# A chunked-attention and low-rank-mixer kernel: values of one tile and scores of the next issued together in shared PSUM banks

## The chip, the cores and the metric

One Trainium2 chip, one of its cores. The metric is the device time of one execution in microseconds (us); less is better. The core has five engines that run side by side and wait for each other through semaphores: TensorE (PE: matmuls; PEld is its weight load, which overlaps them), VectorE (DVE), ScalarE (ACT), GpSimd (POOL) and SyncE (SP, which here only issues DMAs). Matmul results land in PSUM, eight banks of 128 partitions by 512 floats; everything else lies in SBUF.

## The reference

```python
# attention within chunks of 64 positions; q, k, v are (8, 8, 576, 64)
scores = (q_c @ k_c.T) / sqrt(64)
scores = scores - max(scores, axis=-1)
attn = exp(scores)
attn = attn / (sum(attn, axis=-1) + 1e-9)
x = attn @ v_c                        # as (8, 576, 512): batch, seq, heads * dim

# mixer on x
h = x.transpose @ U @ V               # over the 576 positions, rank 32
u = x + h.transpose
out = u + relu(u @ w_ch1) @ w_ch2     # 512 -> 2048 -> 512
```

U, V, w_ch1 and w_ch2 arrive as float64 and are turned into pairs of shorter numbers (a high part and the rest), so that a product is made of three or four matmuls.

## The kernel before

**Tiles.** The batch is cut into four pairs of batch entries (`pr` = 0 to 3). A pair has 1152 rows, which are nine tiles (`t` = 0 to 8) of 128 rows. There are 36 tiles; a tile has two chunks of 64 rows (`c`) and eight heads, which are four head pairs (`hp`) of two (`e`).

**Attention of a tile** (`attention_ops`, line 367). Six groups of operations: load q, k, v; `tq`, `cq`: four TensorE transposes of q into a bank (L375) and their copy to SBUF on ScalarE (L385); `tk`, `ck`: the same for k; `sc`, `m0`, `s0`, `m1`, `s1`, `ex`: the scores (L393), for each `e` maximum (L407) and subtraction (L411) on VectorE, exp on ScalarE (L415); `te`, `ce`: transposes of the exp tile and their copy; `av`, `sm`, `x0`, `x1`: the values (L424), the sums (L436, L437) and the scaled results (L442) that make the tile's `x`.

Scores and values are 32 matmuls each, one for every `(hp, e, c)` of `BLOCKS`. Each uses a quarter of the TensorE array: 64 contraction rows (chosen by `e`) by 64 output columns (chosen by `c`). All other matmuls of the kernel use the whole 128 by 128 array. Scores go to two banks, one for each `e`; values go to two other banks. v has a 65th column of ones, set by a POOL memset (L346), so that the values' 65th output column is the row sum of the exps.

**Mixer.** `project_ops` (xh, xl, y) forms x.transpose @ U for one batch entry from five tiles; `mix_ops` (u, x, ut, uth, utl) adds the low-rank part and transposes; then, for each group `g` of three tiles and each of 16 slices `f` of the 2048 hidden columns, `hidden` (L567, twelve matmuls), `relu_high` on ScalarE (L575), `relu_low` on VectorE (L580) and `project_out` (L593, nine matmuls in three flushes `j`).

**What sets the order.** Pair 0, and tiles 0 and 1 of pair 1, are placed by a planner (`order`). From there on the loop over `plan()` (line 757) writes the order: for each `(pr, g)` it runs the 16 slices and lays a list of steps (attention of later tiles, projections, mixes) evenly between the flushes. `attend` (line 718) makes the attention steps of a list of tiles. Within one list the transposes of the previous tile's exps and its values stand between the steps of the next tile; at the end of each list the last tile's `te` and `av` steps close it:

```python
steps += [ahead, step(*q)] + ([prev[0]] if prev else [])
steps += [step(*k)] + ([prev[1]] if prev else []) + [step(*sc)]
...
return steps + (list(prev) if prev else [])
```

The instructions that result need not stand in the order of these lines: the builder places an instruction on its engine when its own estimate of the run says that what it needs is there, the earlier line first. Buffers with the tag `slot` (eight) hold q, k, v, their transposes, the exps and xh, xl; `bank` has eight, of which three hold the running sums of `project_out`.

Of the kernel before, what the change touches and what calls it, by code (L numbers as in the profile page):

```python
# [10 lines left out]
F32 = mybir.dt.float32  # L11
# [4 lines left out]
AX = mybir.AxisListType  # L16
# [5 lines left out]
def kernel(  # L22
# [11 lines left out]
    nc = tc.nc  # L34
    B, H, S, D = q.shape
# [4 lines left out]
    P = 128  # L40
    C = 64
    D1 = D + 1
    HP = H // 2
    NCC = DM // P
    NF = DF // P
    NT = 2 * S // P
# [2 lines left out]
    NX = 10  # L49
    NS = 8  # L50
    XROOM = 3
    BLOCKS = [(hp, e, c) for hp in range(HP) for e in range(2) for c in range(2)]
    GN = GT * P
    NG = NT // GT
# [6 lines left out]
    work = ctx.enter_context(tc.tile_pool(name="work", bufs=1))  # L61
# [4 lines left out]
    def bank(name):  # L66
        return psum.tile([P, 512], F32, tag="bank", name=name)

    def slot(dtype, name, shape=(P, 512)):
        return work.tile(list(shape), dtype, tag="slot", name=name, bufs=NS)  # L70
# [209 lines left out]
    def w_ops(f, after=None):  # L280
# [10 lines left out]

        n = 1 if f < NF - XROOM else 2
        size = 2 * DM // n
# [33 lines left out]
    def early(pr, t):  # L327
        return pr == 0 and t < NEARLY

    loaded = {}  # L330
    begun = {}
    x_of = {}
    y_of = {}
    ut_of = {}

    def load_qk(pr, t):
        n = f"{pr}_{t}"
        if early(pr, t):
            words = wslot((4 * DM,), F32, "qkv_" + n)
            qn, kn = (words[:, z * DM : (z + 1) * DM].rearrange("p (h d) -> p h d", h=H) for z in range(2))  # L340
            vn = words[:, 2 * DM : 2 * DM + H * D1].rearrange("p (c a k) -> p c a k", c=2, k=D1)
        else:
            qn = slot(F32, "qn_" + n, (P, H, D))
            kn = slot(F32, "kn_" + n, (P, H, D))
            vn = slot(F32, "vn_" + n, (P, 2, HP, D1))
        nc.gpsimd.memset(vn[:, :, :, D:], 1.0)  # L346
        for r, m, b, s0 in segments(pr, t):
            nc.sync.dma_start(qn[r : r + m], q[b, :, s0 : s0 + m, :].rearrange("h s d -> s h d"))
            nc.sync.dma_start(kn[r : r + m], k[b, :, s0 : s0 + m, :].rearrange("h s d -> s h d"))
        loaded[pr, t] = qn, kn, vn  # L350
# [16 lines left out]
    def attention_ops(pr, t, after=None):  # L367
        n = f"{pr}_{t}"
        st = {}
# [7 lines left out]
        def evacuate(name):  # L377
            if name[0] == "e" or not mine:
                dst = slot(F32, name + n, (P, HP, P))
            elif name[0] == "q":  # L380
                st["qk"] = wslot((2, HP, P), F32, "qkT_" + n)
                dst = st["qk"][:, 0]
            else:
                dst = st["qk"][:, 1]
            nc.scalar.copy(dst.rearrange("p a b -> p (a b)"), st[name])  # L385
            st[name] = dst

        def scores():
            ps = [bank(f"sc{e}_{n}") for e in range(2)]
            for hp, e, c in BLOCKS:  # L390
                rows = slice(e * C, (e + 1) * C)
                cs = slice(c * C, (c + 1) * C)
                nc.tensor.matmul(  # L393
                    ps[e][cs, hp * C : (hp + 1) * C],
                    lhsT=st["qT_"][rows, hp, cs],
                    rhs=st["kT_"][rows, hp, cs],
                    start=True,
                    stop=True,
                )
            st["sc"] = [p[:, 0 : HP * C].rearrange("p (h k) -> p h k", k=C) for p in ps]  # L400
# [12 lines left out]
        def exp():  # L413
            exf = st["ex"].rearrange("p a b k -> p (a b k)")
            nc.scalar.activation(exf, exf, AF.Exp, scale=SCALE)  # L415

        def values():

            vn = loaded[pr, t][2]
            ps = [bank(f"av{e}_{n}") for e in range(2)]  # L420
            for hp, e, c in BLOCKS:
                rows = slice(e * C, (e + 1) * C)
                cs = slice(c * C, (c + 1) * C)
                nc.tensor.matmul(  # L424
                    ps[e][cs, hp * D1 : (hp + 1) * D1],
                    lhsT=st["eT_"][rows, hp, cs],
                    rhs=vn[rows, c, hp, :],
                    start=True,
                    stop=True,
                )  # L430
            st["av"] = [p[:, 0 : HP * D1].rearrange("p (h k) -> p h k", k=D1) for p in ps]
# [7 lines left out]
        def scaled(e):  # L439
            if e == 0:  # L440
                st["x"] = work.tile([P, HP, 2, D], F32, tag="x", name="x_" + n, bufs=NX)
            nc.vector.tensor_mul(  # L442
                st["x"][:, :, e, :],
                st["av"][e][:, :, 0:D],
                st["sm"][:, e].unsqueeze(2).broadcast_to([P, HP, D]),
            )
            if e == 1:
                x_of[pr, t] = st["x"].rearrange("p a b k -> p (a b k)")
# [3 lines left out]
        lq = Op("SP", 2.5, lambda: load_qk(pr, t), after, take="w" if mine else "slot slot slot", lat=2.2)  # L452
        lv = Op("POOL" if mine else "SP", 4.0 if mine else 2.5, lambda: load_v(pr, t), lq, lat=2.2)
        tq = Op("PE", 0.35, lambda: transpose(src(0), "qT_"), lq, begun.get((pr, t - 2)), take="bank")
        cq = Op("ACT", 0.58, lambda: evacuate("qT_"), tq, take="w" if mine else "slot", free="bank")
        tk = Op("PE", 0.35, lambda: transpose(src(1), "kT_"), lq, tq, take="bank")
        ck = Op("ACT", 0.58, lambda: evacuate("kT_"), tk, cq, take="" if mine else "slot", free="bank")
        sc = Op("PE", 0.62, scores, ck, take="bank bank", free="w" if mine else "slot slot slot slot")
        m0 = Op("DVE", 0.41, lambda: maximum(0), sc, take="slot mx")
        s0 = Op("DVE", 0.41, lambda: subtract(0), m0, free="bank")  # L460
        m1 = Op("DVE", 0.41, lambda: maximum(1), s0)
        s1 = Op("DVE", 0.41, lambda: subtract(1), m1, free="bank mx")
        ex = Op("ACT", 0.63, exp, s1)
        te = Op("PE", 0.35, lambda: transpose(flat(), "eT_"), ex, take="bank", free="slot")
        ce = Op("ACT", 0.58, lambda: evacuate("eT_"), te, take="slot", free="bank")
        av = Op("PE", 0.65, values, ce, lv, take="bank bank x", free="slot w" if mine else "slot slot")
        sm = Op("DVE", 0.5, sums, av, take="sm")
        x0 = Op("DVE", 0.415, lambda: scaled(0), sm, free="bank")
# [176 lines left out]

    LEAD = "T0 T1 U T2 T3 T4 P0 V W0 M0 T5 W1 T6 T7 W2 T8 P1 M1 W3 W4 W5 W6 W7 W8 W9 W10 W11 W12 W13 W14 W15 M2"
    STRETCHES = ((0, 0, 2), (1, 0, 4), (0, 2, 8), (1, 4, 12), (0, 8, 16), (1, 12, 16))
    GATES = (14, 29)
    BASE = 1000
    u_done = None  # L650
    v_done = []
# [25 lines left out]
    prev = None  # L677
    blocks = 0
    gates = dict(zip(GATES, range(len(GATES))))
    for g, f0, f1 in STRETCHES:  # L680
        for f in range(f0, f1):
            rank[0] = BASE
            prev = block_ops(0, g, f, f == f0, f == f1 - 1, [*w_done[f], *mixed[g]], prev)
# [31 lines left out]
    def step(*group):  # L715
        return lambda: [o.run() for o in group]

    def attend(ts):
        steps = []
        prev = None  # L720
        for key in ts:
            i = tiles.index(key)
            _, q, k, sc, et, av = attention_ops(*key)

            def ahead(i=i):
                if i + 1 < len(tiles) and tiles[i + 1] not in loaded:
                    load(*tiles[i + 1])

            steps += [ahead, step(*q)] + ([prev[0]] if prev else [])
            steps += [step(*k)] + ([prev[1]] if prev else []) + [step(*sc)]  # L730
            prev = step(*et), step(*av)
        return steps + (list(prev) if prev else [])

    def mixes(pr, ts):
        steps = []
        st = [[step(*z) for z in mix_ops(pr, t, None, [None, None])] for t in ts]
        for i in range(len(st) + 1):
            steps += ([st[i][0]] if i < len(st) else []) + ([st[i - 1][1]] if i else [])
        return steps

    def proj(pr, e):
        return [step(*z) for z in project_ops(pr, e, [None] * NT)[0]]

    def plan():
        n1 = len(GATES)
        for pr in range(NPAIR):
            nxt = [] if pr == NPAIR - 1 else [(pr + 1, t) for t in range(NT)]
            if pr > 0:
                yield pr, 0, attend([(pr, t) for t in range(7, NT)]) + proj(pr, 1) + mixes(
                    pr, range(3, 6)  # L750
                ) + attend(nxt[:1])
                yield pr, 1, mixes(pr, range(6, 9)) + attend(nxt[1:4])
            yield pr, 2, attend(nxt[n1 if pr == 0 else 4 : 5]) + ([] if not nxt else proj(pr + 1, 0)) + attend(nxt[5:7]) + (
                [] if not nxt else mixes(pr + 1, range(3))
            )

    for pr, g, steps in plan():
        done = 0
        slots = 0
        for f in range(NF):  # L760
            ps = hidden(pr, g, f)
# [43 lines left out]
```

## Time and profile before

| | before |
|---|---|
| median of 3 runs | 1030.82 us |
| range of the runs | 1030.47 to 1032.12 us |
| span of the profiled execution, first to last instruction | 1032.0 us |
| attention tiles from pair 1, tile 2 on | 25 |
| PE matmuls | 7032 |

The profiled execution's time is its span of 1032.0 us; the page gives no other for it. It lies 1.2 us above the median of the runs and within their range.

How to read it: the page gives the busy time of each engine, the span in 40 slices with the busy share in tenths, the chain of work that ended last, and groups of instructions by line. In a row of groups, `L393 PE MATMUL sc<-kT,qT 64*64 64x64 f32 x864 | busy, mean ns | idle before` means line 393, TensorE, output sc from kT and qT, 64 rows by 64 columns of the array, a 64x64 moving operand, 864 times. A row of the timeline gives start, length, engine, line, operation and how many in a row. A matmul's end is modelled, and matmuls overlap, so what matters on TensorE is the distance between starts. `[0.28 <-ACT ex L415]` behind a row says that the engine sat idle that long before it and who ended the wait.

### The profile page before, as it was taken

To read this page: it belongs to the slowest core of one execution; us is meant where nothing else is said; L and a number is where in the kernel's file an instruction comes from. 1 tells how busy PE (TensorE), PEld (TensorE's weight loads), DVE (VectorE), ACT (ScalarE), POOL (GpSimd) and SP (SyncE) were. 2 spreads that over 40 slices of the span, in tenths; PEclk is the share of its full clock that TensorE was granted. 3 is DMA by queue.
4 is the path that set the end of the run, shared out by engine and by line. 5 is a ranking of instruction groups with operands and counts; after the bars stand their busy time and mean duration, and the time that the engine had idled before them with its cause. 6 is when DMAs were issued, how large, how long until landed. Compare 5 with 4: busy or idle time off the path is not lost.

```text
span 1032.0 us, 16637 instructions
## 1 busy us (share of the span) xinstructions
PE 980.7 (95%) x7032; PEld 862.0 (84%) x7032; DVE 419.5 (41%) x834; ACT 260.8 (25%) x467; POOL 26.4 (3%) x78
## 2 busy tenths in 40 slices
PE   5486999999999999999999999999999999999998
PEld 4364888888888888988888888988888889999997
DVE  3498999973333342322423242322333332211211
ACT  3453234322322222222222222222222231111110
POOL 7100000000000000000000000000000000000000
PEclk9667899999999999999999999999999999999999
DMA  9952142305121211021021210111121000000000
GB/s 187 217 184 88 42 113 82 103 34 129 34 63 31 63 31 32 34 55 37 32 62 32 62 32 10 53 34 43 48 53 41 31 1 1 31 1 1 31 1 30
DMA packets 123157, 56.40 MB, mean 55 GB/s; under 512 B 107276, under 2 KB 115724, under 8 KB 123084
## 3 DMA queue, kind: packets, MB, share of 16 engines
q1 hardware_dynamic: 121932, 52.99, 20.1%
q0 software_dynamic: 1152, 2.36, 1.2%
q8 instruction: 55, 0.90, 0.4%
q14 instruction: 18, 0.15, 0.0%
HBM read 45.83 MB, written 9.51 MB: 54 GB/s over the span
## 4 chain that ended last, share of the span: by engine, by line
PE 69%; DVE 0%; ACT 0%; DVEq 0%; issue 0%; ACTq 0%
PE h L567 30%; PE o L593 30%; PE av L424 1%; PE sc L393 1%; PE ut L535 1%; PE ps_eT L375 1%; PE ps_kT L375 1%; PE ps_qT L375 1%; PE u L523 1%; PE y L496 1%; PE y L495 1%; DVE x L605 0%; DVE ex L411 0%; ACT ex L415 0%; DVEq L800 0%; DVE mx L407 0%
## 5 line engine op out<-in xcount | busy, mean ns | idle before, releaser
L567 PE MATMUL h<-uth,w 128*128 128x384 f32 x1536 | 427.1, 342 | 4.9 <-ACT w L308 2.1
L593 PE MATMUL o<-w,hh 128*128 128x512 f32 x1152 | 364.3, 403 | 0.6 <-ACT hh L575 0.6
L567 PEld LDWEIGHTS h<-uth,w 128*128 128x128 f32 x1536 | 282.4, 189 | 13.8 <-ACT w L308 2.6
L580 DVE SCALAR_TENSOR_TENSOR hl<-h,hh 128x384 fp32r<-128x384 f32 x192 | 106.8, 556 | 430.4 <-ACT hh L575 430.4
L567 PE MATMUL h<-utl,w 128*128 128x384 f32 x768 | 260.2, 339 | 0.4 <-DVE utl L548 0.4
L593 PEld LDWEIGHTS o<-w,hh 128*128 128x128 f32 x1152 | 207.8, 189 | 35.8 <-ACT hh L575 0.9
L593 PE MATMUL o<-w,hl 128*128 128x512 f32 x576 | 217.9, 395 | 0.0
L575 ACT ACTIVATE hh<-h 128x384 fp32r<-128x384 f32 x192 | 94.3, 491 | 477.3 <-PE h L567 477.2
L567 PEld LDWEIGHTS h<-utl,w 128*128 128x128 f32 x768 | 144.9, 189 | 6.6 <-DVE utl L548 0.6
L593 PEld LDWEIGHTS o<-w,hl 128*128 128x128 f32 x576 | 108.2, 188 | 25.0 <-DVE hl L580 0.3
L375 PE MATMUL ps_eT<-ident,ex 128*128 128x128 f32 x144 | 24.8, 301 | 25.0 <-ACT ex L415 25.0
L415 ACT ACTIVATE ex<-ex 128x512 f32<-128x512 f32 x36 | 22.7, 632 | 89.7 <-DVE ex L411 89.1
L375 PEld LDWEIGHTS ps_eT<-ident,ex 128*128 128x128 f32 x144 | 18.9, 153 | 31.1 <-ACT ex L415 27.9
L407 DVE TENSOR_REDUCE mx<-sc 128x4 f32<-128x256 f32 x72 | 28.0, 418 | 37.7 <-PE sc L393 37.7
L488 DVE TENSOR_TENSOR xl<-x,xh 128x512 fp32r<-128x512 f32 x40 | 27.2, 687 | 29.6 <-ACT xh L484 25.6
L529 DVE TENSOR_TENSOR x<-u,x 128x512 f32<-128x512 f32 x36 | 24.1, 684 | 26.7 <-PE u L523 26.4
L548 DVE TENSOR_TENSOR utl<-ut,uth 128x512 fp32r<-128x512 f32 x36 | 24.5, 690 | 25.2 <-ACT uth L543 25.1
L605 DVE TENSOR_TENSOR x<-o,x 128x512 f32<-128x512 f32 x48 | 31.2, 685 | 7.7 <-PE o L593 7.6
L543 ACT CAST uth<-ut 128x512 fp32r<-128x512 f32 x36 | 20.9, 587 | 40.4 <-PE ut L535 36.6
L385 ACT COPY eT<-ps_eT 128x512 f32<-128x512 f32 x36 | 21.1, 586 | 39.4 <-PE ps_eT L375 39.4
L484 ACT CAST xh<-x 128x512 fp32r<-128x512 f32 x40 | 24.1, 621 | 17.8 <-PE y L496 7.5
L411 DVE TENSOR_TENSOR ex<-sc,mx 128x256 f32<-128x256 f32 x72 | 28.0, 417 | 0.8
(74 smaller groups left out, 590.2 us busy)
## 6 DMA issues: line engine op xcount, KB each, us to landing
wraw<-in_moe_w_ch_dram SPq DMA_DIRECT2D x32, 512.0 KB, 4.5
out_dram<-x SPq DMA_DIRECT2D x36, 256.0 KB, 2.1
vn<-in_v_dram SPq DMA_DIRECT2D x108, 64.0 KB, 2.9
qn<-in_q_dram SPq DMA_DIRECT2D x24, 256.0 KB, 3.3
kn<-in_k_dram SPq DMA_DIRECT2D x24, 256.0 KB, 4.1
qkv<-in_v_dram POOLq DMA_DIRECT2D x36, 64.0 KB, 6.3
qkv<-in_q_dram SPq DMA_DIRECT2D x8, 256.0 KB, 9.4
qkv<-in_k_dram SPq DMA_DIRECT2D x8, 256.0 KB, 7.6
```

The lines of the kernel that those rows point to most:

```text
L375: nc.tensor.transpose(ps[:, j * P : (j + 1) * P], src[:, j * P : (j + 1) * P], ident)
L407: nc.vector.reduce_max(mx, st["sc"][e], axis=AX.X)
L411: nc.vector.tensor_sub(st["ex"][:, :, e, :], st["sc"][e], mx.unsqueeze(2).broadcast_to([P, HP, C]))
L484: nc.scalar.copy(st["h"], x_of[pr, i + 4 * e])
L488: nc.vector.tensor_sub(st["l"], x_of[pr, i + 4 * e], st["h"])
L529: nc.vector.tensor_add(x, st["u"], x)
L548: nc.vector.tensor_sub(ul[:, :, js], st["t"].rearrange("p (c t) -> p c t", c=NCC), uh[:, :, js])
L567: nc.tensor.matmul(ps[:, :GN], lhsT=w[:, z, cc], rhs=u[:, cc, :], start=(n == 0), stop=(n == 3 * NCC - 1))
L575: nc.scalar.activation(hh, ps[:, :GN], AF.Relu)
L580: nc.vector.scalar_tensor_tensor(hl, ps[:, :GN], 0.0, hh, op0=ALU.max, op1=ALU.subtract)
L593: nc.tensor.matmul(acc[j], lhsT=h[:, js], rhs=w2[f][:, z], start=(first and i == 0), stop=(final and i == 2),)
L605: nc.vector.tensor_add(x, ps, x)
```

## The change

For every tile from pair 1, tile 2 on (those for which `lone` is false):

- the values of a tile and the scores of the next tile are issued one after the other in one step (`both`), into the same two banks: scores in columns 0 to 255, values in columns 256 to 511 of bank `e`;
- v has no column of ones any more (64 columns, no POOL memset); the row sums are a VectorE reduction over the exps (`row_sums`), with the same addition of 1e-9 and reciprocal;
- `attend` no longer closes its list: the last tile waits for the next list (`waiting`), so all 25 tiles form one chain; `rest()` ends it in pair 3;
- the lists are cut elsewhere: five of a tile's steps instead of six, and a tile more before the projections that need its predecessor.

Pair 0 and tiles 0 and 1 of pair 1 stay as they were; the constant `GATES` only moves up.

```diff
+    GATES = (14, 29)
...
+    def lone(pr, t):
+        return pr == 0 or (pr == 1 and t < len(GATES))
...
-            vn = slot(F32, "vn_" + n, (P, 2, HP, D1))
-        nc.gpsimd.memset(vn[:, :, :, D:], 1.0)
+            vn = slot(F32, "vn_" + n, (P, 2, HP, D1 if lone(pr, t) else D))
+        if lone(pr, t):
+            nc.gpsimd.memset(vn[:, :, :, D:], 1.0)
...
         def scores():
-            ps = [bank(f"sc{e}_{n}") for e in range(2)]
+            ps = st.get("pair") or [bank(f"sc{e}_{n}") for e in range(2)]
...
+        def row_sums():
+            sm = st["sm"] = work.tile([P, HP, 2], F32, tag="sm", name="sm_" + n, bufs=2)
+            nc.vector.reduce_sum(sm, st["ex"], axis=AX.X)
+            nc.vector.tensor_scalar_add(sm, sm, 1e-9)
+            nc.vector.reciprocal(sm, sm)
+
+        def values_beside(other):
+
+            vn = loaded[pr, t][2]
+            ps = [bank(f"as{e}_{n}") for e in range(2)]
+            for hp, e, c in BLOCKS:
+                rows = slice(e * C, (e + 1) * C)
+                cs = slice(c * C, (c + 1) * C)
+                nc.tensor.matmul(
+                    ps[e][cs, (HP + hp) * C : (HP + hp + 1) * C],
+                    lhsT=st["eT_"][rows, hp, cs],
+                    rhs=vn[rows, c, hp, :],
+                    start=True,
+                    stop=True,
+                )
+            st["av"] = [p[:, HP * C :].rearrange("p (h k) -> p h k", k=D) for p in ps]
+            if other is not None:
+                other["pair"] = ps
...
         def scaled(e):
...
+            sm = st["sm"][:, e] if lone(pr, t) else st["sm"][:, :, e]
             nc.vector.tensor_mul(
                 st["x"][:, :, e, :],
                 st["av"][e][:, :, 0:D],
-                st["sm"][:, e].unsqueeze(2).broadcast_to([P, HP, D]),
+                sm.unsqueeze(2).broadcast_to([P, HP, D]),
             )
...
+        if not lone(pr, t):
+            rs = Op("DVE", 0.9, row_sums, ex, take="sm")
+            beside[pr, t] = st, values_beside, scaled
+            begun[pr, t] = te
+            return [[lq, lv], [tq, cq], [tk, ck], [sc, m0, s0, m1, s1, ex, rs], [te, ce]]
...
+    waiting = [None]
+
     def attend(ts):
         steps = []
-        prev = None
         for key in ts:
             i = tiles.index(key)
-            _, q, k, sc, et, av = attention_ops(*key)
+            _, q, k, sc, et = attention_ops(*key)
...
-            steps += [ahead, step(*q)] + ([prev[0]] if prev else [])
-            steps += [step(*k)] + ([prev[1]] if prev else []) + [step(*sc)]
-            prev = step(*et), step(*av)
-        return steps + (list(prev) if prev else [])
+            prev, waiting[0] = waiting[0], key
+            steps += [ahead, step(*q)] + ([step(*turn_of[prev])] if prev else [])
+            steps += [step(*k), both(prev, key, sc)]
+            turn_of[key] = et
+        return steps
+
+    turn_of = {}
+
+    def both(prev, key, sc):
+        def run():
+            if prev:
+                st, values, scaled = beside[prev]
+                values(beside[key][0] if key else None)
+            if key:
+                sc[0].run()
+            if prev:
+                scaled(0)
+                scaled(1)
+            for o in sc[1:]:
+                o.run()
+
+        return run
+
+    def rest():
+        prev, waiting[0] = waiting[0], None
+        return [step(*turn_of[prev]), both(prev, None, [])]
...
-                yield pr, 0, attend([(pr, t) for t in range(7, NT)]) + proj(pr, 1) + mixes(
+                yield pr, 0, attend([(pr, 8)]) + (attend(nxt[:1]) if nxt else rest()) + proj(pr, 1) + mixes(
                     pr, range(3, 6)
-                ) + attend(nxt[:1])
+                )
                 yield pr, 1, mixes(pr, range(6, 9)) + attend(nxt[1:4])
-            yield pr, 2, attend(nxt[n1 if pr == 0 else 4 : 5]) + ([] if not nxt else proj(pr + 1, 0)) + attend(nxt[5:7]) + (
+            yield pr, 2, attend(nxt[n1 if pr == 0 else 4 : 6]) + ([] if not nxt else proj(pr + 1, 0)) + attend(nxt[6:8]) + (
                 [] if not nxt else mixes(pr + 1, range(3))
             )
```

More of the change, by code (lines that the diff above doesn't have):

```diff
@@ L328, in early @@
         return pr == 0 and t < NEARLY
+    def lone(pr, t):
+        return pr == 0 or (pr == 1 and t < len(GATES))
     loaded = {}
     begun = {}
+    beside = {}
     x_of = {}
@@ L647 @@
     STRETCHES = ((0, 0, 2), (1, 0, 4), (0, 2, 8), (1, 4, 12), (0, 8, 16), (1, 12, 16))
-    GATES = (14, 29)
     BASE = 1000
```

## The prediction, made before the changed kernel ran

> **What bounds the kernel now.** I read the page first (busy times, the slices, the chain that ended last), then a table by stretch of the part that the change touches, then the waits there, and last the timeline around single blocks of scores and values.
>
> ```profile
> PE 980.7 (95%) x7032; PEld 862.0 (84%) x7032; DVE 419.5 (41%) x834; ACT 260.8 (25%) x467; POOL 26.4 (3%) x78
> ...
> PE   5486999999999999999999999999999999999998
> ...
> PE 69%; DVE 0%; ACT 0%; DVEq 0%; issue 0%; ACTq 0%
> ```
>
> TensorE is the busiest engine, is below nine tenths only in the first four slices (about 100 us), and carries the chain that ended last. A busy share alone says little, since the ends of matmuls are modelled; so the stretch in which the 25 changed tiles run:
>
> ```profile
> 231.00:320.00 89.00, 88.44 (x804) 76.22 (x803) 30.88 (x81) 24.70 (x46) 0.68 (x6) 0.95 0.33 76
> ...
> 400.00:480.00 80.00, 80.00 (x617) 70.46 (x616) 23.99 (x57) 17.82 (x33) 0.45 (x4) 0.95 0.19 44
> 480.00:560.00 80.00, 80.00 (x615) 70.36 (x614) 24.98 (x60) 18.97 (x36) 0.34 (x3) 0.95 0.19 46
> ...
> PEld sc L393 <- issue: 8.6, 26, 0.4
> PEld av L424 <- issue: 8.1, 26, 0.4
> PE ps_eT L375 <- ACT ex L415: 0.6, 2, 0.3
> ```
>
> The columns of the first three are the stretch, its length, then PE, PEld, DVE, ACT and POOL busy (with instructions), the granted clock (0.95 throughout), the DMA share and GB/s; the last three rows are waits (total, times, longest). PE has no idle time from 400 us on; DVE is busy 24 to 25 us of 80. In 231 to 850 us PE proper waits twice, 0.3 us each, for an exp. But its weight load sits idle 0.3 us before nearly every block of scores and of values, ended by "issue", that is by nothing the profile names: no data was missing. So time on PE is the bound, and those entries are time that PE loses by itself.
>
> **The merged blocks.** One block of scores and one of values, with their neighbours on PE:
>
> ```profile
> 401.32 0.40 PE L593 MATMUL o<-w,hh 128*128 128x512 f32 x1
> 401.65 0.69 PE L393 MATMUL sc<-kT,qT 64*64 64x64 f32 x32
> 402.28 0.50 PE L593 MATMUL o<-w,hh 128*128 128x512 f32 x1
> 402.62 0.39 PE L593 MATMUL o<-w,hl 128*128 128x512 f32 x1
> 402.85 0.39 PE L593 MATMUL o<-w,hh 128*128 128x512 f32 x1
> ...
> 407.15 0.34 PE L567 MATMUL h<-utl,w 128*128 128x384 f32 x1
> 407.32 0.34 PE L567 MATMUL h<-uth,w 128*128 128x384 f32 x1
> 407.59 0.70 PE L424 MATMUL av<-vn,eT 64*64 64x65 f32 x32
> 408.21 0.44 PE L567 MATMUL h<-uth,w 128*128 128x384 f32 x1
> 408.50 0.33 PE L567 MATMUL h<-utl,w 128*128 128x384 f32 x1
> ...
> L424 PE MATMUL av<-vn,eT 64*64 64x65 f32 x864 | 18.8, 224 | 0.0
> L393 PE MATMUL sc<-kT,qT 64*64 64x64 f32 x864 | 18.8, 225 | 0.0
> ```
>
> Undisturbed, o matmuls start 0.23 us apart (402.62 to 402.85), h matmuls 0.17 (407.15 to 407.32). From the last o before the scores to the second after them is 402.62 - 401.32 = 1.30 us; without the block it would be 2 x 0.23 = 0.46. The block of scores costs PE 0.84 us. For the values: 408.50 - 407.32 - 2 x 0.17 = 0.84 (0.83 with unrounded steps). Inside a block the matmuls overlap: busy 0.69 less one matmul's own 0.225 leaves 0.47 us for 31 steps, 15 ns a matmul; for the values 0.48, 15 to 16 ns. So 32 matmuls are worth 0.49 us, and the other 0.33 to 0.35 us of each block is entering and leaving the quarter-array form: part before it (401.32 to 401.65 where 0.23 is usual), most behind (the first full-size matmul after it has 0.34 us to its successor, not 0.23). Values and scores in one run of 64 enter and leave once: one 0.33 is saved per junction. The 25 tiles of the chain have 24 junctions (first scores and last values stand alone): 24 x 0.33 = 7.9 us, all of it PE time where PE is never idle, hence off the end. The moving operand of the values shrinks from 65 to 64 columns; the two rows differ by 1 ns the other way, so I count nothing.
>
> The trace has one place, in the lead at the same clock, where two blocks already stand together:
>
> ```profile
> 20.02 0.69 PE L393 MATMUL sc<-qkT 64*64 64x64 f32 x32 [0.71 <-ACT qkT L385]
> 20.53 0.77 PE L424 MATMUL av<-qkv,eT 64*64 64x65 f32 x32
> 21.23 0.66 PE L375 MATMUL ps_qT<-ident,qkv 128*128 128x128 f32 x4
> ```
>
> The values start 0.51 us after the scores did, which is 32 steps of 16 ns: no seam. They then take 0.77 instead of 0.70 us, so a second block can cost 0.07 or 0.08 more than the first. There the values came second and their operands had only just landed; in the change the scores come second, with operands written earlier. I take no extra, and keep 24 x 0.08 = 1.9 us for the range.
>
> **The closed lists.** Before, the last tile of each list has its exp transposes one step behind its scores:
>
> ```profile
> 276.41 0.70 PE L393 MATMUL sc<-kT,qT 64*64 64x64 f32 x32
> ...
> 278.55 0.86 PE L593 MATMUL o<-w,hl 128*128 128x512 f32 x3
> 279.02 0.63 ACT L415 ACTIVATE ex<-ex 128x512 f32<-128x512 f32 x1 [2.01 <-DVE ex L411]
> 279.70 0.66 PE L375 MATMUL ps_eT<-ident,ex 128*128 128x128 f32 x4 [0.28 <-ACT ex L415]
> ```
>
> Three o from 278.55 end their turn at 279.24; the transposes start at 279.70: 0.46 us lost, and the wait row above counts two such. In the chain three steps lie between, so both should go: 0.9 us. What is late next is nothing on PE, unless the longer chain below is. I take half, 0.5 us, because the placement of these steps changes anyway.
>
> **Row sums on VectorE.**
>
> ```profile
> L407 DVE TENSOR_REDUCE mx<-sc 128x4 f32<-128x256 f32 x72 | 28.0, 418 | 37.7 <-PE sc L393 37.7
> ...
> L548 DVE TENSOR_TENSOR utl<-ut,uth 128x512 fp32r<-128x512 f32 x36 | 24.5, 690 | 25.2 <-ACT uth L543 25.1
> ...
> L436 DVE TENSOR_SCALAR sm<-av 128x4 f32<-128x4 f32 x72 | 8.1, 154 | 29.7 <-PE av L424 29.7
> ...
> DVE hl L580 <- ACT hh L575: 305.5, 108, 5.7
> ```
>
> A reduction of 128x512 lies between 0.69 us (another operation of that size) and 0.84 (twice the 128x256 reduction). One of the two small additions goes (0.15). Net 0.54 to 0.69 us a tile, 25 tiles: 14 to 17 us more on DVE. It waits for the exp, and hl (L580), which o needs, can be queued behind it; but DVE waited 305.5 us in 108 times just for the input of hl, 2.8 us each, so I count nothing. If that cover were gone it would cost the 14 to 17 us. The 25 POOL memsets removed, with the v loads on SP behind them, cost PE nothing now.
>
> **New waits.** The scores' first weight load now waits for kT one step after its transposes, and every later matmul stands behind it:
>
> ```profile
> 396.68 0.61 PE L375 MATMUL ps_kT<-ident,kn 128*128 128x128 f32 x4
> ...
> 397.33 0.58 ACT L385 COPY kT<-ps_kT 128x512 f32<-128x512 f32 x1 [1.25 <-PE ps_kT L375]
> ```
>
> kT is there 397.91 - 396.68 = 1.23 us after the transposes start. Between lie the rest of the transposes (0.35), at least one flush of three o (0.7) and the values themselves (0.5): 1.55. Enough, barely. And the exp comes later: VectorE may read the shared banks only when both blocks are written, and scales the values first: 0.5 + 2 x 0.42 us (the L407 size) later than now. In the row above an exp is ready 3.24 us after its scores start (279.65 - 276.41), so 4.6 us after a merged block starts; the transposes that need it are three steps away, some 5 us in the tightest list (41 steps over 58 places of about 1.2 us). I count nothing, again with little to spare. Two banks are held for about 4 us instead of two pairs for about 2 each: nothing.
>
> **Sum.** 7.9 + 0.5 = 8.4 us, less 0.3 for one junction that does not come about: 8.1. The profiled execution's span of 1032.0 would become 1023.9; it lies 1.2 above the median of 1030.8, so the forecast is a median of 1022.7 us.
>
> **Rivals.**
>
> *The second half is not there in time.* In the steady part, PE's instructions queue up while large matmuls run, so 32 small ones start as from a full store; the following 32 come at the pace at which the sequencer hands them over. The row at 20.53 may show that pace: 0.08 us more. Then 24 x (0.33 - 0.08) = 6.0, and the median is 1030.8 - 6.0 - 0.5 = 1024.3 with the lists counted. The Trainium skill, "TensorE: Matmul & The Clock Gate", gives a queue depth of 64 in its table of specifications (32 weight loads and 32 matmuls by count) and, under "Wait — 56ns, not 53.3ns?", about 25 ns as the least distance between starts. By an estimate with that page's 25 ns a second 32 would cost 0.8 us, only 0.04 less than alone, and the change would gain about 1 us. The rows above with 15 ns for 32 in a row speak against that floor here, and so does 0.77 us for the second block.
>
> *The builder parts the two.* The order on the engine isn't the source's: at 401.65 the scores stand between two o of one flush. Where kT is late in the builder's estimate, values go first and o or h follow before the scores. Each such junction forfeits 0.33. With half of them parted, 4 us and the 0.5 of the lists are left: 1026.3. With all, the change does not do what it says, and the median stays at 1030.3 to 1031.
>
> *Slower: PE waits for the exp in every tile.* If the longer VectorE chain (4.6 us) meets transposes placed closer than that, each tile pays as at 279.70, 0.46 us and up. 24 x 0.46 = 11.0 against 7.9: +3, a median of 1034. The gain is gone from 0.33 us a tile. For it speaks how small the spare is; against it, that within the lists before, three steps were always enough (only two waits of PE for an exp in 25 tiles, both at the end of a list).
>
> **How the numbers follow.** The forecast (most junctions made, 7 to 9.3 us gained): 0.64. The slower second half (5 to 7): 0.14. Parted junctions (2 to 5): 0.10. Nothing: 0.04. Slower: 0.08. 2 us, 0.2%, is about what a measurement of this kernel can tell from no change. So faster 0.88, same 0.04, slower 0.08. The range begins at 24 x 0.35 + 0.9 = 9.3 and a little for the order: 1021.0; it ends at 1026.8, half of the junctions parted and nothing from the lists. That leaves out the nothing, the slower and a part of the parted: 0.18.
>
> **What would show it.** In the profile after: runs of values x32 followed at once by scores x32, 24 of them, their starts 0.5 us apart; the scores' busy 0.69 if the second half keeps pace, 0.77 if not; about 25 entries of 0.3 us by "issue" instead of 52; no wait of PE for an exp; DVE about 435 us; PE busy throughout to an end 8 us earlier. Wrong it would be if other matmuls stand between, if the second block runs slower than 20 ns a matmul, or if PE shows idle time in front of the exp transposes or scores.

## The result

| | before | changed |
|---|---|---|
| median | 1031.47 us | 1023.19 us |
| range | 1030.47 to 1032.59 | 1021.47 to 1024.96 |
| ratio, 95% interval | | 0.9914 (0.9898 to 0.9930) |
| the same pair on another occasion | 1032.64 us | 1022.53 us, ratio 0.9901 (0.9884 to 0.9918) |

The changed kernel takes 8 to 10 us less; 1022.7 was forecast. (A run's time is 1.7 to 2.1 us longer than the span of the same execution: 1021.47 us and 1019.7 for the changed kernel's profile, which is the fastest of its four runs. By an estimate from this, the profiled execution of before, with its span of 1032.0, lay about 3 us above the median of 1030.82, not 1.2, and so the two spans differ by more than the medians.) First the page after, for the lines shown of before:

```profile
PE 967.9 (95%) x7032; PEld 857.0 (84%) x7032; DVE 432.8 (42%) x834; ACT 259.8 (25%) x467; POOL 23.7 (2%) x53
...
PE   5476999999999999999999999999999999999998
...
PE 85%; DVE 1%; ACT 0%; issue 0%; DVEq 0%; ACTq 0%
```

PE does the same 7032 matmuls in 12.8 us less busy time. Part of what a visit costs had counted as busy: the first full-size matmul behind a block is drawn longer (0.50 us at 402.28 in the profile of before, where 0.39 is usual). DVE has 13 us more. PE still bounds. The table by stretch (same columns as before), then all waits of PE or its weight load from 231 to 850 us:

```profile
231.00:320.00 89.00, 88.86 (x851) 78.22 (x850) 37.38 (x91) 26.27 (x50) 0.00 (x0) 1.00 0.36 82
...
400.00:480.00 80.00, 80.00 (x596) 71.60 (x595) 24.18 (x53) 16.46 (x31) 0.00 (x0) 1.00 0.17 40
480.00:560.00 80.00, 80.00 (x656) 70.98 (x655) 30.97 (x67) 22.22 (x41) 0.00 (x0) 1.00 0.21 50
...
PEld as L436 <- issue: 7.7, 23, 0.4
PEld sc L399 <- issue: 0.6, 2, 0.4
PEld ps_eT L381 <- ACT ex L421: 0.4, 1, 0.4
PEld as L436 <- ACT hh L611: 0.4, 1, 0.4
PEld as L436 <- ACT xh L520: 0.4, 1, 0.4
PEld av L454 <- issue: 0.3, 1, 0.3
```

Before, 52 blocks were entered with such an idle time, all that there are in this stretch. Now there are 28 entries at such blocks: 24 junctions, the chain's first scores and last values, and the two blocks of the one lone tile in it. The two waits of PE for an exp are gone. One new wait for an exp has come, which this view lists only for the weight load:

```profile
263.22 0.60 PE L381 MATMUL ps_qT<-ident,qn 128*128 128x128 f32 x4
263.96 0.65 PE L381 MATMUL ps_eT<-ident,ex 128*128 128x128 f32 x4
```

The four transposes of q start 0.11 us apart, the last at 263.55; the first transpose of the exps starts 0.41 us later, so 0.3 us is lost. One junction from the timeline of PE:

```profile
437.60 0.63 PE L629 MATMUL o<-w,hh 128*128 128x512 f32 x2
438.06 0.40 PE L629 MATMUL o<-w,hl 128*128 128x512 f32 x1
438.39 0.69 PE L436 MATMUL as<-vn,eT 64*64 64x64 f32 x32
438.91 0.65 PE L399 MATMUL as<-kT,qT 64*64 64x64 f32 x32
439.48 0.44 PE L603 MATMUL h<-uth,w 128*128 128x384 f32 x1
439.76 0.34 PE L603 MATMUL h<-utl,w 128*128 128x384 f32 x1
```

Values and scores stand in one run, 0.52 us from start to start. From the o at 438.06 to the second h behind, 1.70 us, less one o step (0.23) and one h step (0.17): 1.30 for both, 1.29 with unrounded starts. Two blocks alone cost 2 x 0.82. So a junction is worth 0.35 to 0.36 us. All 24 junctions of the chain are of this form. (The source has 16 matmuls for each block, and each stands twice in the trace: 32 rows. Where the text ahead of the prediction says 32 for the `(hp, e, c)`, read 16.)

Where in the span is the gain? The lead (all that stands ahead of the loop over `plan()`, which the change leaves alone) ends in every profile with the same wait of PE for hh; its time, and the last rows of PE, before and after:

```profile
220.04 0.73 PE L593 MATMUL o<-w,hh 128*128 128x512 f32 x2 [0.58 <-ACT hh L575]
...
1026.51 0.86 PE L593 MATMUL o<-w,hl 128*128 128x512 f32 x3
```

```profile
217.92 0.73 PE L629 MATMUL o<-w,hh 128*128 128x512 f32 x2 [0.58 <-ACT hh L611]
...
1014.17 0.86 PE L629 MATMUL o<-w,hl 128*128 128x512 f32 x3
```

Between the two rows lie 806.47 us before and 796.25 after: 10.2 us less. The other 2.1 us of the 12.3 by which the spans differ (1032.0 and 1019.7) come from the lead, where nothing was changed. Of the 10.2, 24 x 0.355 = 8.5 are the junctions; the two waits for an exp that are gone give 0.9, and the new one takes 0.3.

The 1.1 us that are left go with the profile of before. It is a little slower throughout than the other nine: within a group of four, transposes of k start 110.3 ns apart on average, in the others 108.7 to 108.8. Its granted clock reads 0.95, theirs 1.00 (from 231 us on); that the clock is the reason isn't shown. A fairer measure is the kernel of "The row sums alone" below, which has no junction and, but for 38 of 5648 matmuls, the order of before on PE. Its profile, at 1.00, takes 805.22 us for this stretch:

```profile
219.07 0.73 PE L608 MATMUL o<-w,hh 128*128 128x512 f32 x2 [0.58 <-ACT hh L590]
...
1024.29 0.86 PE L608 MATMUL o<-w,hl 128*128 128x512 f32 x3
```

The changed kernel is 9.0 us shorter than that, and the parts make it up: 8.5 for the junctions, 0.8 for two waits for an exp that this kernel has too, less 0.3.

### The profile page after: what moved, and what is told of

Same layout as the page of the kernel before. It is cut to its first block, busy times and chain, and to the rows that moved or that the text cites. A ratio compares the mean times of both kernels' runs of the same rounds, so it can differ in the third digit from the quotient of the medians.

```text
span 1019.7 us, 16488 instructions
## 1 busy us (share of the span) xinstructions
PE 967.9 (95%) x7032; PEld 857.0 (84%) x7032; DVE 432.8 (42%) x834; ACT 259.8 (25%) x467; POOL 23.7 (2%) x53
## 4 chain that ended last, share of the span: by engine, by line
PE 85%; DVE 1%; ACT 0%; issue 0%; DVEq 0%; ACTq 0%
PE o L629 38%; PE h L603 38%; PE as L436 2%; PE ps_kT L381 1%; PE ut L571 1%; PE ps_eT L381 1%; PE as L399 1%; PE ps_qT L381 1%; PE y L531 1%; PE u L559 1%; PE y L532 1%; PE sc L399 0%; ACT hh L611 0%; DVE x L641 0%; PE av L454 0%; DVE wraw L101 0%
## 5 line engine op out<-in xcount | busy, mean ns | idle before, releaser
L629 PE MATMUL o<-w,hl 128*128 128x512 f32 x576 | 224.8, 396 | 0.0
L473 DVE TENSOR_TENSOR x<-as,sm 128x256 f32<-128x256 f32 x50 | 20.9, 419 | 41.9 <-PE as L399 41.9
L309 ACT CAST w<-wroom 128x1024 fp32r<-128x1024 f32 (+1 forms) x19 | 17.2, 913 | 32.9 <-DVE wroom L102 29.9
```

What stands on the lines that cost most here:

```text
L629: nc.tensor.matmul(acc[j], lhsT=h[:, js], rhs=w2[f][:, z], start=(first and i == 0), stop=(final and i == 2),)
```

## The experiments

The theory: each separate visit to the quarter-array form costs PE about 0.36 us beyond its matmuls, and everything else in the change is free. The rivals: the gain comes from the rest of the change (one chain, no column of ones, row sums), from the shared banks, or the change would cost VectorE time that only luck covers. All ratios are to the kernel before, run on the same chip.

**Apart again.** The changed kernel, with values (`first`) and scores with all that follows them (`second`) as two steps of the list.

```diff
-            steps += [step(*k), both(prev, key, sc)]
+            steps += [step(*k), *both(prev, key, sc)]
...
-        return run
+        return [first, second] if prev and key else [lambda: (first(), second())]
```

> The changed kernel with values and scores as two steps of the list instead of one; banks, row sums and the chain stay. 17 of the 24 junctions come apart (other matmuls stand between), 7 stay. Seam theory (each separate visit to the quarter-array form costs TensorE about 0.36 us beyond its matmuls): 17 x 0.36 = 6.1 us more than the changed kernel, some 2.2 us less than the kernel before, ratio to it about 0.998. Rival (the gain comes from the rest: one chain, no closed lists, no column of ones, row sums ahead of the values): about the time of the changed kernel, ratio 0.992.

Measured: 1031.23 us, ratio 0.9986 (0.9977 to 0.9995). The count in the expectation was wrong: the trace shows 20 junctions apart and 4 kept. One that is apart, on PE:

```profile
441.91 0.33 PE L603 MATMUL h<-uth,w 128*128 128x384 f32 x1
442.17 0.69 PE L436 MATMUL as<-vn,eT 64*64 64x64 f32 x32
442.80 0.73 PE L629 MATMUL o<-w,hh 128*128 128x512 f32 x2
...
444.05 0.39 PE L629 MATMUL o<-w,hl 128*128 128x512 f32 x1
444.37 0.69 PE L399 MATMUL as<-kT,qT 64*64 64x64 f32 x32
445.00 0.73 PE L629 MATMUL o<-w,hh 128*128 128x512 f32 x2
```

Each block has its own way in (0.32 us from an o, where 0.23 is usual) and its own way out. 20 x 0.355 = 7.1 us. The two rows that bound the stretch behind the lead:

```profile
220.73 0.73 PE L629 MATMUL o<-w,hh 128*128 128x512 f32 x2 [0.58 <-ACT hh L611]
...
1024.40 0.86 PE L629 MATMUL o<-w,hl 128*128 128x512 f32 x3
```

That is 803.67 us, 7.4 longer than in the changed kernel (796.25). 0.8 of it is a wait of PE for a kT that the changed kernel hasn't, and the changed kernel's 0.3 for an exp is missing here; this leaves 6.9 for the 20 junctions. That one edit returns most of the gain, with chain, banks and row sums unchanged. Against the 805.22 us of the row sums alone it is 1.55 shorter: 4 kept junctions (1.4), two waits for an exp that are gone (0.8), the wait for a kT (-0.8). So next to nothing is left over for the other cutting of the lists, which no run takes out alone.

**The row sums alone.** The kernel before, with 64 columns of v and the row sums on VectorE for the 25 tiles.

```diff
...
+        if not lone(pr, t):
+            rs = Op("DVE", 0.9, row_sums, ex, take="sm")
+            return [[lq, lv], [tq, cq], [tk, ck], [sc, m0, s0, m1, s1, ex, rs], [te, ce], [av, x0, x1]]
```

> The kernel before with the row sums on VectorE and 64 columns of v for the same 25 tiles, nothing else. Seam theory: VectorE has the room, so no difference, ratio 0.999 to 1.001. Rival (the gain comes from the row sums and the missing memsets): most of the 8 us, ratio 0.992 to 0.995. If the extra VectorE time of 14 us were not covered: up to 1.013.

Measured: 1032.13 us, ratio 0.9993 (0.9985 to 1.0002). VectorE's busy time is 435.2 us, 15.7 more than before, and the time stays: neither a gain from the missing memsets and the shorter rows of v, nor a cost, beyond the interval (1.5 us less to 0.2 more). Behind the lead its profile is 1.25 us shorter than that of before; transposes, which the row sums don't touch, are faster in it too, and how much of the 1.25 belongs to the row sums isn't separated. It can't be most of the gain.

**Scores twice.** The changed kernel issues the matmuls of the scores a second time, into the same place (the same values overwrite themselves).

```diff
-            for hp, e, c in BLOCKS:
+            for hp, e, c in BLOCKS * (2 if "pair" in st else 1):
```

> The changed kernel with the 32 matmuls of the scores issued twice, into the same place, at each of the 24 junctions: runs of 96 instead of 64. Seam theory: a further 32 in the same visit cost their matmuls alone, 0.46 to 0.49 us, so 24 x 0.47 = 11 us more than the changed kernel, ratio to the kernel before about 1.003. If a block cost its full 0.82 us wherever it stands: 20 us more, ratio 1.011. If supply fails beyond the first 64 instructions (second and third 32 slower): the third block would show well over 16 ns a matmul in the trace.

Measured: 1033.7 us, ratio 1.0013 (1.0004 to 1.0023), 10 to 12 us above the changed kernel by the ratios (0.9914 and 0.9901). Behind the lead its profile takes 807.37 us, 11.1 more than the changed kernel's. The same junction on PE:

```profile
442.32 0.40 PE L629 MATMUL o<-w,hl 128*128 128x512 f32 x1
442.65 0.69 PE L436 MATMUL as<-vn,eT 64*64 64x64 f32 x32
443.17 1.11 PE L399 MATMUL as<-kT,qT 64*64 64x64 f32 x64
444.21 0.44 PE L603 MATMUL h<-uth,w 128*128 128x384 f32 x1
444.49 0.34 PE L603 MATMUL h<-utl,w 128*128 128x384 f32 x1
```

From the o to the second h now 2.17 us instead of 1.70: 32 more matmuls in the same visit cost 0.47 us, not 0.82; 24 x 0.47 = 11.2 us. The 64 of the scores start within 1.11 - 0.22 = 0.89 us, 14 ns apart. So no supply runs dry, neither in the second block nor in the third.

**Banks of their own.** The changed kernel, with the scores in two other banks.

```diff
-            if other is not None:
-                other["pair"] = ps
```

> The changed kernel with values and scores still issued together, but the scores in two banks of their own. All 24 junctions stay. Seam theory: the time of the changed kernel, ratio 0.992, unless TensorE waits for banks (four held by a tile instead of two; with three sums and one or two for the hidden layer there are just eight). If the shared banks themselves are what helps: close to the kernel before, ratio 0.998 to 1.0.

Measured: 1021.49 us, ratio 0.9896 (0.9878 to 0.9914), which overlaps the changed kernel's intervals. All 24 junctions stay, and PE shows no wait for a bank from 231 to 850 us. The shared banks are not needed for the gain.

**Only together.** Chain and adjacency, and nothing else but the lists as the changed kernel cuts them: banks of their own, the column of ones and its memset back, sums from the 65th column.

```diff
-            vn = slot(F32, "vn_" + n, (P, 2, HP, D1 if lone(pr, t) else D))
+            vn = slot(F32, "vn_" + n, (P, 2, HP, D1))
...
-                    ps[e][cs, (HP + hp) * C : (HP + hp + 1) * C],
+                    ps[e][cs, hp * D1 : (hp + 1) * D1],
```

> The one chain with values and scores issued together, and nothing else of the change: the scores in banks of their own, the column of ones and its memset back, the sums from the values' 65th column. All 24 junctions stay. Seam theory: the whole gain, ratio 0.990 to 0.992. Rival (shared banks or row sums on VectorE carry part of it): ratio nearer to 1.

Measured: 1023.6 us, ratio 0.9915 (0.9899 to 0.9931): the whole gain.

**The sums twice.** The changed kernel does each row-sum reduction twice, the second over the first.

```diff
             nc.vector.reduce_sum(sm, st["ex"], axis=AX.X)
+            nc.vector.reduce_sum(sm, st["ex"], axis=AX.X)
```

> The changed kernel with the row-sum reduction done twice in each of the 25 tiles (the second overwrites the first with the same values). It adds some 25 x 0.7 = 17 us to VectorE. Theory that VectorE's work is covered: the time of the changed kernel, ratio to the kernel before 0.990 to 0.992. Rival (the row sums lie on TensorE's path, through hl or the transposes of the exps): up to 17 us more, ratio up to 1.008, with waits of TensorE for VectorE in the trace.

Measured: 1023.78 us, ratio 0.9915 (0.9899 to 0.9931). Its page and the reductions:

```profile
PE 970.2 (95%) x7032; PEld 858.8 (84%) x7032; DVE 448.6 (44%) x859; ACT 260.1 (25%) x467; POOL 23.8 (2%) x53
...
L425 DVE TENSOR_REDUCE sm<-ex 128x8 f32<-128x512 f32 x25 | 17.1, 685 | 13.3 <-ACT ex L421 12.7
L426 DVE TENSOR_REDUCE sm<-ex 128x8 f32<-128x512 f32 x25 | 17.0, 681 | 0.4
```

VectorE is busy 448.6 us instead of 432.8, with 17.0 in the added reduction, and the time stays: the cover holds twice the load.

**Closed lists.** The changed kernel closes each list of attention steps again, as before.

```diff
-        return steps
+        return steps + (rest() if ts else [])
...
-                yield pr, 0, attend([(pr, 8)]) + (attend(nxt[:1]) if nxt else rest()) + proj(pr, 1) + mixes(
+                yield pr, 0, attend([(pr, 8)]) + (attend(nxt[:1]) if nxt else []) + proj(pr, 1) + mixes(
```

> The changed kernel with each list of attention steps closed again (the last tile's exp transposes and values stand at its end, with no scores behind them). 12 of the 24 junctions stay. Seam theory: 12 x 0.36 = 4.3 us more than the changed kernel, plus up to 0.4 us for each list end at which TensorE waits for the exp (13 ends), so 4 to 9 us more, ratio to the kernel before 0.996 to 1.000. Rival (the one chain adds nothing over the junctions inside the lists): about the time of the changed kernel, ratio 0.991.

Measured: 1031.1 us, ratio 0.9990 (0.9981 to 0.9998), near the upper end of the expectation. 12 junctions are kept. A list's end on PE:

```profile
286.36 0.62 PE L629 MATMUL o<-w,hh 128*128 128x512 f32 x2
286.82 0.40 PE L629 MATMUL o<-w,hl 128*128 128x512 f32 x1
287.80 0.66 PE L381 MATMUL ps_eT<-ident,ex 128*128 128x128 f32 x4 [0.58 <-ACT ex L421]
289.19 0.69 PE L436 MATMUL as<-vn,eT 64*64 64x64 f32 x32 [0.73 <-ACT eT L391]
```

The stretch behind the lead:

```profile
221.51 0.73 PE L629 MATMUL o<-w,hh 128*128 128x512 f32 x2 [0.58 <-ACT hh L611]
...
1025.26 0.86 PE L629 MATMUL o<-w,hl 128*128 128x512 f32 x3
```

At the list's end PE stands still for the exp (0.98 us from the o to the transposes, where 0.23 is usual) and for the copy of its transposes. Behind the lead the profile takes 803.75 us, 7.5 longer than that of the changed kernel: 12 x 0.355 = 4.3 for the junctions, 1.9 for four waits at transposes of an exp that the changed kernel hasn't (as distances between starts beyond the usual step), 0.7 for the wait in the last row, 0.6 not followed. So closing the lists gives back most of the gain: the one chain makes half of the junctions, and it keeps the exp's users three steps away.

**The changed kernel again**, beside the last three.

> The changed kernel itself, beside the three others on the same chip: ratio 0.990 to 0.993 by every theory; it sets the scale for the others.

Measured: 1022.53 us, ratio 0.9901 (0.9884 to 0.9918).

## Why the prediction was right, point by point

- **PE is the bound, so time saved on PE is saved at the end:** right. PE loses 0.3 us to a wait between 231 and 850 us after. Its busy row stands at nine tenths in all slices but the first four and the last, as before (the prediction names only the first four).
- **24 x 0.33 = 7.9 us for the junctions:** the mechanism is right, shown by taking 20 junctions apart (6.9 us of the 7.4 that come back) and by leaving only chain and adjacency in (whole gain). The size is a little low: 0.355 each, 8.5. The prediction gave the second block 0.49 us, 32 steps of the first block's mean; it costs 0.47. In the traces the starts of a visit come in fours, 7 ns apart, with 38 ns from one four to the next; only from the first four to the second it is 87 ns (medians over the blocks), and the 49 ns more are paid once a visit.
- **0.07 to 0.08 us more for a second block** (the end of the range, from the one pair in the lead): not there. The scores behind the values take 0.65 us, not 0.77. Why the second block in the lead was slower (the prediction names operands that had only just landed) isn't shown.
- **0.5 us for the closed lists:** 0.6 came. Both waits are gone (0.9), and one new wait for an exp takes 0.3 back. The closed lists put back cost more than these two waits; at the list's end shown above, the later exp of a merged block meets its transposes one step behind.
- **Nothing for VectorE:** right; 15.7 us more in the kernel before, and 16 more still in the changed one, cost nothing. The reduction took 0.69 us, the lower of the two bounds; DVE 432.8 where 435 was expected.
- **One junction lost (0.3 us):** none was.
- **kT just in time, and the exp 4.6 us behind:** in the changed kernel PE never waits for kT from 231 to 850 us; in the kernel with values and scores apart there is one wait of 0.8 us for a kT, so the small spare was real. The exp is ready 3.9 to 4.0 us after a merged block starts, not 4.6: the 3.24 us from which the prediction started is one of the longer times before, where most lie near 2.8. The count of nothing held for the exp at all tiles but one (0.3 us).
- **Rivals:** a slower second half fell with the third block at 14 ns a matmul. The Trainium skill, "TensorE: Matmul & The Clock Gate", section "Wait — 56ns, not 53.3ns?", gives about 25 ns as the least distance between starts. That isn't the floor for these overlapping quarter-array matmuls. Parted junctions did not occur, though the experiment shows how easily they do. PE waiting for the exp in every tile did not occur either: the changed kernel has one such wait, the one with lists closed four more.
- **The number:** that the median came so close to 1022.7 is in part luck. The sum was 8.1 us, without the full size of the junctions and with one of them lost; the stretch behind the lead gained 9.0, or 10.2 against the profile of before. The medians differ by 8.3 on one occasion and 10.1 on the other, and the lead alone ends between 217.9 and 222.5 us in the ten profiles.

Not settled: what in the array makes the visit cost 0.36 us. The Trainium skill, "TensorEngine Tiling (Array Packing)", section "Key Properties", says that a change of the tiling mode drains TensorE. The way in and out seen here (0.36 us a visit) agrees with that, but no run separates a drain from a weight load that can't be hidden.

## What to carry to other kernels

Where PE is never idle, look at the distance between matmul starts around blocks of another array shape: what exceeds the usual step is the price of the visit, and it is paid per visit, not per matmul. Put such blocks of different tiles next to each other, and lay the order so that the later ones' operands are ready without a pause; sharing banks is not what matters. When attention steps are laid out in lists, don't close the lists: their ends put dependent steps next to each other and cost both a visit and a wait.

## What the runs showed of the hardware

- Beyond the usual steps of its neighbours, a visit to the quarter-array form costs PE 0.82 us with 32 rows of matmuls (the 52 blocks of before), 1.29 with 64 (the 24 junctions of the changed kernel) and 1.76 with 96 (the same with the scores twice). So each 32 rows cost 0.47 and the visit itself 0.36.
- From the end of the lead on, the kernel repeats to a hundredth of a microsecond (796.25 us in one profile of the changed kernel, 796.26 in the next, whose rows follow), while the lead itself ended at 217.9 in one and 222.2 in the other. What differs between these profiles lies in the first fifth of the kernel, so a change behind it is read more sharply from a stretch than from whole times.

```profile
222.20 0.73 PE L629 MATMUL o<-w,hh 128*128 128x512 f32 x2 [0.58 <-ACT hh L611]
...
1018.46 0.86 PE L629 MATMUL o<-w,hl 128*128 128x512 f32 x3
```

- The granted clock stands at 0.95 in the profile of before and at 1.00 in that of after, yet o matmuls start 0.23 us apart in both. What goes with that difference in the record is small: transposes of k start 110.3 ns apart and not 108.7, and the stretch behind the lead takes about 1 us of 806 more than the changes account for.
